# Attention with a gated feed-forward on one core: masked queries by transfers, a load count for spare matmuls, and traced transfer times

## The chip, the cores and the metric

The kernel runs on one core of a Trainium2 chip. Its engines are TensorE (PE in the profile; its weight loads are PEld), VectorE (DVE), ScalarE (ACT), GpSimd (POOL) and SyncE (SP), which here only issues transfers (DMAs). The metric is the time of one execution on the device in microseconds. Three runs of the kernel before took 1190.16, 1193.30 and 1193.92 us; their median is 1193.3.

## The reference

```python
x  = A_x                                   # [1, 2048, 512], bf16
xn = _layernorm(x)
qkv = (xn @ wqkv).reshape(B, S, 3, H, Dh)  # H = 32 heads of Dh = 16
scores = einsum("bhqd,bhkd->bhqk", q, k) * Dh ** -0.5
p = softmax(scores)                        # over 2048 keys
o = einsum("bhqk,bhkd->bhqd", p, v)
attention = o.reshape(B, S, D) @ wo        # wo: 512 x 512
h = silu(xn @ w1) * (xn @ w3)              # 512 -> 1792
feed_forward = h @ w2                      # 1792 -> 512
return x + attention + feed_forward
```

Inputs and output are bf16.

## The kernel before

**Units.** Queries are cut into 4 chunks of 512 and heads into 8 groups of 4. A chunk and a group are worked off in units of 256 queries, the first group in 128, 128, 256 and the last four groups in 128 each: 73 units. Four heads of 16 dimensions lie in four bands of 32 partitions of `QT` and `KT`; a band has 16 rows of data, then two rows that hold minus the maximum of each query (as a bf16 number and its rest) in `QT` and ones in `KT`; the other rows of `QT` are zero.

**First scores.** For each unit PE computes scores with queries on partitions (L1158, two heads of 512 keys at a time, each on 32 rows of the array), and DVE takes the maximum over each 512 keys (`tensor_reduce`, L1197, 128x1024 at a time). There are 1004 such reductions, and 10 more are done by another DVE operation (L1186) on a unit that ACT has helped to halve. PE has two places of 2 banks of PSUM for them, so it can be at most two ahead of DVE.

**Maxima to rows.** When the last reduction of a unit is done, POOL joins the partial maxima in six small operations (L1323 to L1330), writes minus the maximum and its rest into `Z` (L1300, L1302), and SP issues a transposing transfer `Zs<-Z` (L1346) and two transfers `QT<-Zs` (L1342) that put the rows into `QT`. After that the unit's second scores may begin.

**Second scores.** PE computes the scores again with keys on partitions and the maximum already subtracted, in one of two ways: one head on 32 rows of the array (L1447, four heads side by side), or "wide", all 128 rows, with a copy of the queries that is zero outside one head's band: `BD` (L661 and L665, inputs `BD,KT`). `BD` has two buffers, by the unit's parity, of four heads each. POOL makes it by multiplying `QT` with a column of `hmask` (L1284), one operation per head, after the rows of `QT` have landed. A wide matmul is used only where its mask is ready in the plan and PE's load is low, or where it fits.

**Exponentials and values.** ACT takes the exponential of a bank of 512 (L1472) or two banks at once (L1502) into `PT`. PE multiplies with the values and a column of ones (`PT,Vaug`, L665), which gives the unnormalized output and the sum; ACT copies it to `U` (L1566), and the normalization follows: transfer `Lc<-U` (L1587), reciprocal on POOL (L1591), transfer `rd<-Rc` to DRAM (L1596), transfer `R<-rd` back, spread over partitions (L1600), multiply on POOL (L1611).

**Other work of PE** is put between: transposes and projections of the inputs at the start, the feed-forward (tiles G and U, with three POOL operations per tile, L939 to L943), output sums OUT (OUTA and OUTB at the end), and spare matmuls (`fill_cand`), whose results nobody reads: they are placed where a running sum over the last 2 us, `heat`, is below `HEAT_FILL`. A weight per kind of matmul goes into it (`_HEAT_ROW`, `_HEAT_COL`, `_HEAT_FULL`). Where `heat` is below `HEAT_P1`, first scores are computed twice or three times over.

**The order** of every engine, SP's included, is written out by a planner inside `_build` before the program is made. It keeps a clock per engine, gives each item an `occ` (time on its engine) and a `lat` (time until others see its result; 2.3 us for a transfer unless another is given), and always takes the item that can begin first. For each 24 score tiles one of 53 sets of rule parameters (`SETS`) applies, by a list (`TUNE`). On the chip an engine follows its written order and waits at each item until what it needs is there; so a time that the planner has wrong does not make a wrong result, it makes a wait, and everything behind it on that engine waits too.

**The start**: x comes in four transfers, and layer norm's mean and variance are taken on DVE (`bn_stats`, L698) for the tile pairs marked "d" in `STATS`, on ACT (L688, L692) for those marked "a".

The clock per transfer, in the planner:

```python
def later_dma(fn, reads, writes, lat=2.3, cb=None, pred=None, occ=0.62):
    spq.append(_Item(fn, reads, writes, occ, lat, cb, pred))
```

Of the kernel before, what the change touches and what calls it, by code (L numbers as in the profile page):

```python
# [5 lines left out]
FP32 = mybir.dt.float32  # L6
# [8 lines left out]
_HEAT_ROW, _HEAT_COL, _HEAT_FULL = 0.794, 2.36, 2.16  # L15
# [22 lines left out]
class _Prog:  # L38
# [99 lines left out]
    def pe(self, fn, reads, writes, mode, groups, dur, name="", first=None):  # L138
# [19 lines left out]
        w = _HEAT_ROW * len(groups) if mode == "row" else _HEAT_FULL if self.pe_full else _HEAT_COL  # L158
        self.heat.append((start, start + dur, w))
# [98 lines left out]
def _build(nc, A_x, A_wqkv, A_wo, B_w1, B_w3, B_w2, out):  # L258
# [28 lines left out]
    AUG_LAT = 3.8  # L287
# [17 lines left out]
    BD_END = 4  # L305
    SPLIT_LO = 20
# [13 lines left out]
        dict(A_LEAD=0.85),  # L320
        dict(TOL=0.05),
        dict(TOL=0.15),
        dict(PV_LEFT=2),
        dict(PV_LEFT=8),
        dict(TEN_MID=2),
        dict(RELAX=0.05),
        dict(MIN_PIECE=2),
        dict(BD_NEAR=0.1),
        dict(BD_NEAR=0.5),
        dict(HEAT_FILL=0.0),  # L330
        dict(HEAT_FILL=2.0),
        dict(HEAT_WIDE=0.0),
# [6 lines left out]
        dict(A_LEAD=0.95, PV_LEFT=8, ROW_LEAD=0.43, PAIR_TEN=2),  # L339
        dict(ROW_LEAD=0.43, LAZY_GAP=0.02),  # L340
        dict(TOL=0.05, TEN_MID=2),
        dict(LAZY_GAP=0.02, ROW_LEAD=0.5, RELAX=0.05),
        dict(HEAT_P1=1.5, RELAX=0.05, PAIR_WAIT=0.1),
        dict(TEN_MID=2, ROW_LEAD=0.55),
        dict(HEAT_TILE=1.6, HEAT_FILL=3.0),
        dict(MIN_PIECE=2, MATE=0.0, WIDE_LEAD=0.7, HEAT_FILL=2.0),
        dict(RELAX=0.05, MATE=0.0, PAIR_WAIT=0.1, W_WAIT=0.1),
        dict(LAZY_GAP=0.02, TOL=0.15, HEAT_FILL=2.0, A_LEAD=0.69),
        dict(PAIR_WAIT=0.1, HEAT_FORCE=1.0, HEAT_WIDE=1.15, HEAT_P1=1.5),
        dict(LAZY_GAP=0.02, WIDE_LEAD=1.0, MATE=0.0),  # L350
        dict(TEN_MID=2, RELAX=0.05, LAZY_GAP=0.02, HEAT_WIDE=1.15),
        dict(MIN_PIECE=2, HEAT_FILL=2.0, LAZY_GAP=0.02, PAIR_WAIT=0.1),
        dict(HEAT_WIDE=1.4, PAIR_WAIT=0.1, PV_LEFT=8, HEAT_TILE=1.3),
        dict(MIN_PIECE=2, BD_NEAR=0.1, W_WAIT=0.1),
        dict(HEAT_TILE=1.3, MIN_PIECE=2),
        dict(BD_NEAR=0.1, HEAT_P1=0.0),
        dict(ROW_LEAD=0.55, RELAX=0.05, MATE=0.0),
        dict(ROW_LEAD=0.43, A_LEAD=0.85, HEAT_WIDE=0.0),
        dict(BD_NEAR=0.5, ROW_LEAD=0.5),
        dict(HEAT_TILE=1.6, PAIR_TEN=2, ROW_LEAD=0.55, HEAT_FILL=3.0),  # L360
        dict(HEAT_TILE=1.3, TOL=0.05, HEAT_FILL=1.15),
        dict(PAIR_TEN=0, WIDE_LEAD=1.0),
        dict(W_WAIT=0.1, TEN_MID=2, WIDE_LEAD=1.0),
        dict(ROW_LEAD=0.4, HEAT_FILL=2.0),
    )
    TUNE = (
# [73 lines left out]
    with ctx:  # L440
# [35 lines left out]
        hmask = sb("hmask", [128, 4], FP32)  # L476
# [64 lines left out]
        poolq = {k: [] for k in ("z", "ln", "nx", "split", "bd", "nrm", "ffn", "pad")}  # L541
# [23 lines left out]
        P.op("dve", lambda e: e.memset(hmask[:, :], 0.0), writes=[("hmask",)], occ=0.07)  # L565

        def head_masks(e):
            for j in range(4):
                ins = e.memset(hmask[32 * j:32 * j + 32, j:j + 1], 1.0)
            return ins  # L570
        P.op("dve", head_masks, writes=[("hmask",)], occ=0.26)
# [9 lines left out]
        NORM = "dddppppp"  # L581
        STATS = "ddddaaaa"
# [58 lines left out]
        wpad = {k: v.rearrange("p (c j) d -> p c (j d)", c=DC) for k, v in wpad.items()}  # L641
        poolq["pad"].append(_Item(lambda e: e.memset(Vaug[:, :, :, 16:17], 1.0), [],
# [36 lines left out]
        def ln_chunk(gi):  # L679
# [6 lines left out]
            if on_act:  # L686
                for t in tl:
                    act_stats.append(_Item(lambda e, t=t: e.activation(  # L688
                        a32[:, :], x_sb[:, t, :], ACTF.Identity, scale=1.0 / D, accum_out=mv[:, t, 0:1]),
                        [("PT", t)], [("a32",), ("mv", t)], 0.57, 0.7))  # L690
                for t in tl:
                    act_stats.append(_Item(lambda e, t=t: e.activation(  # L692
                        a32[:, :], x_sb[:, t, :], ACTF.Square, scale=-1.0, bias=mv[:, t, 0:1],
                        accum_out=mv[:, t, 1:2]),
                        [("PT", t), ("mv", t)], [("a32",), ("mv", t)], 0.66, 0.8, cb=lambda op: mv_done(op)))
# [575 lines left out]
        def bd_prep():  # L1271
# [10 lines left out]
            for j in (2, 3, 0, 1):  # L1282
                poolq["bd"].append(_Item(
                    lambda e, j=j: e.tensor_scalar(BD[:, u % 2, j, 0:nq], QT[:, qs, q0:q0 + nq], hmask[:, j:j + 1], 0.0,  # L1284
                                                   ALU.mult, ALU.add),
# [831 lines left out]
```

## Time and profile before

| | us |
|---|---|
| median of three runs | 1193.3 |
| the profiled execution's own time | 1192.82 |
| its span, first to last instruction | 1191.1 |
| DVE busy | 1167.3 |
| ACT busy | 1166.1 |
| PE busy | 1115.3 |
| POOL busy | 576.4 |

The span begins with the first instruction and ends with the last one; 1.7 us of the execution's time lie outside of it. A line such as `L1197 DVE ... part<-ps` is a group of instructions by source line, engine and tile, with its busy time, the mean length of one in ns, and the idle time of the engine just before them. Instructions of ACT and DVE overlap their neighbours a little, so the mean length is more than the distance from one to the next. In a table by stretches each row has the stretch, its length, busy time (and count) of PE, PEld, DVE, ACT and POOL, then the granted TensorE clock as a share of full speed, the share of the DMA engines and GB/s.

### The profile page before, as it was taken

The numbers are of one execution on the slowest core, as the hardware profiler recorded it, in microseconds if no ns is written. First come the engines' busy times: TensorE is split into PE (matmuls) and PEld (weight loads), VectorE is DVE, ScalarE is ACT, GpSimd is POOL, SyncE is SP. The second block draws the span as 40 slices with busy tenths as digits, with TensorE's granted clock in tenths as the row PEclk, the third lists the DMA queues.
The fourth block names the chain that finished last, engine by engine and source line by source line (L and its number), as shares of the span: only waits on it lengthen the run. The fifth ranks groups of instructions, "written<-read, shape, count | busy, mean of one in ns | idle before, by whom it ended". The sixth has DMA issues, their size and how long they took to land.

```text
span 1191.1 us, 35904 instructions
## 1 busy us (share of the span) xinstructions
PE 1115.3 (94%) x14863; PEld 531.2 (45%) x15011; DVE 1167.3 (98%) x1085; ACT 1166.1 (98%) x2259; POOL 576.4 (48%) x1200
## 2 busy tenths in 40 slices
PE   8999999999999999999999999999999999999998
PEld 4443444444444434433444443434444543356664
DVE  8999999999999999999999999999999999999995
ACT  7899999999999999999999999999999999999997
POOL 4457644545443375545354338554543337644430
PEclk9999999999999999999999999999999999999999
DMA  5423221111101121111101112111110112000000
GB/s 183 129 72 87 61 79 52 38 35 29 38 22 34 35 68 38 31 38 29 37 19 30 36 49 55 42 32 33 31 29 25 29 40 51 20 20 18 20 16 24
DMA packets 130790, 52.24 MB, mean 44 GB/s; under 512 B 99788, under 2 KB 130628, under 8 KB 130628
## 3 DMA queue, kind: packets, MB, share of 16 engines
q1 hardware_dynamic: 130628, 49.94, 16.3%
q8 instruction: 118, 1.93, 0.7%
q14 instruction: 44, 0.36, 0.1%
HBM read 38.67 MB, written 6.74 MB: 38 GB/s over the span
## 4 chain that ended last, share of the span: by engine, by line
ACT 56%; PE 23%; DVE 14%; DMA 4%; POOL 2%; issue 1%; SPq 0%; DVEq 0%; POOLq 0%
ACT PT L1472 41%; DVE part L1197 13%; PE ps L661 8%; ACT PT L1502 7%; PE ps L665 6%; PE ps L1447 4%; PE ps L1158 4%; DMA R<-rd 2%; ACT zg L960 1%; DMA rd<-Rc 1%; ACT ub L964 1%; ACT U L1566 1%; ACT th L954 1%; ACT kq L849 1%; POOL BD L1284 1%
## 5 line engine op out<-in xcount | busy, mean ns | idle before, releaser
L1197 DVE TENSOR_REDUCE part<-ps 128x2 f32<-128x1024 f32 x1004 | 1138.5, 1203 | 6.1 <-PE ps L1158 3.7
L1472 ACT ACTIVATE PT<-ps 128x512 bf16<-128x512 f32 x1706 | 918.3, 742 | 4.6 <-PE ps L1447 2.9
L1447 PE MATMUL ps<-QT,KT 32*128 32x256 bf16 (+1 forms) x3338 | 452.7, 258 | 9.6 <-ACT PT L1502 1.8
L1158 PE MATMUL ps<-KT,QT 32*128 32x512 bf16 x2140 | 431.7, 384 | 10.4 <-DVE part L1197 7.6
L1447 PEld LDWEIGHTS ps<-QT,KT 32*128 32x128 bf16 x3338 | 159.2, 92 | 163.0 <-ACT PT L1472 73.6
L665 PE MATMUL ps<-PT,Vaug 128*17 128x256 bf16 (+1 forms) x4672 | 202.4, 262 | 3.3 <-ACT PT L1502 0.9
L1502 ACT ACTIVATE PT<-ps 128x1024 bf16<-128x1024 f32 x171 | 193.3, 1157 | 0.0
L1591 POOL TENSOR_TENSOR Rc<-Lc,mone 128x8 f32<-128x8 f32 (+1 forms) x69 | 105.0, 1521 | 139.2 <-DMA Lc<-U 139.1
L1158 PEld LDWEIGHTS ps<-KT,QT 32*128 32x128 bf16 x2140 | 105.4, 91 | 143.5 <-issue 69.3
L661 PE MATMUL ps<-xnT,w 128*128 128x512 bf16 (+3 forms) x588 | 147.9, 316 | 11.1 <-ACT PT L1472 4.0
L661 PE MATMUL ps<-BD,KT 128*128 128x256 bf16 (+1 forms) x870 | 147.5, 263 | 9.2 <-ACT PT L1502 3.2
L1284 POOL TENSOR_SCALAR BD<-QT,hmask 128x256 bf16<-128x256 bf16 (+1 forms) x276 | 122.2, 457 | 65.6 <-DMA QT<-Zs 65.6
L665 PEld LDWEIGHTS ps<-PT,Vaug 128*17 128x17 bf16 x4672 | 92.9, 90 | 75.9 <-issue 53.9
L661 PE MATMUL ps<-xnT,ident 128*128 128x512 bf16 (+3 forms) x274 | 78.7, 325 | 12.6 <-ACT PT L1502 3.6
L661 PEld LDWEIGHTS ps<-BD,KT 128*128 128x128 bf16 x870 | 68.9, 98 | 43.7 <-ACT PT L1502 7.7
L1323 POOL TENSOR_TENSOR mx<-part 128x16 f32<-128x16 f32 (+1 forms) x67 | 14.1, 211 | 150.2 <-DVE part L1197 149.8
L665 PE MATMUL ps<-BD,KT 128*32 128x256 bf16 (+1 forms) x1856 | 82.9, 265 | 0.0
L661 PEld LDWEIGHTS ps<-xnT,w 128*128 128x128 bf16 x631 | 50.1, 97 | 73.5 <-issue 37.6
L661 PE MATMUL ps<-w,hT 128*128 128x128 bf16 (+3 forms) x330 | 77.3, 302 | 3.9 <-ACT U L1566 3.0
L943 POOL TENSOR_TENSOR hT<-a,t 128x512 bf16<-128x512 f32 x56 | 71.1, 1269 | 2.3
L941 POOL TENSOR_TENSOR a<-zg,ub 128x512 f32<-128x512 bf16 x56 | 64.6, 1153 | 5.1 <-ACT ub L964 4.9
L1611 POOL TENSOR_TENSOR wk_on<-U,R 128x256 bf16<-128x256 f32 (+1 forms) x36 | 22.9, 635 | 79.5 <-DMA R<-rd 79.5
(112 smaller groups left out, 776.9 us busy)
## 6 DMA issues: line engine op xcount, KB each, us to landing
w<-in_B_w_dram SPq DMA_DIRECT2D x112, 128.0 KB
R<-rd SPq DMA_DIRECT2D x55, 128.0 KB
QT<-qd SPq DMA_DIRECT2D x31, 128.0 KB
KT<-kd SPq DMA_DIRECT2D x28, 128.0 KB
PT<-in_A_x_dram SPq DMA_DIRECT2D x4, 512.0 KB
xr<-in_A_x_dram SPq DMA_DIRECT2D x16, 128.0 KB
out_dram<-osb SPq DMA_DIRECT2D x16, 128.0 KB
qd<-kq SPq DMA_DIRECT2D x15, 128.0 KB
```

The lines of the kernel that those rows point to most:

```text
L661: return e.matmul(bank(bk)[:, c0 + a:c0 + b], make_lhsT(0, 128), rhs_ap(0)[:, a:b], start=start, stop=stop, **kw)
L665: ins = e.matmul(bank(bk)[32 * i:32 * i + m, c0 + a:c0 + b], make_lhsT(i), rhs if (a, b) == (0, ncols) else rhs[:, a:b], start=start, stop ...
L941: q.append(_Item(lambda e: e.tensor_tensor(a32[:, :], zg[:, ss, :], ub[:, ss, :], ALU.mult), [("zg", ss), ("ub", ss)], [("a32",)], 1.1, 1.25))
L943: q.append(_Item(lambda e: e.tensor_tensor(hT[:, hslot(idx), :], a32[:, :], t1[:, :], ALU.mult), [("a32",), ("t1",)], [("hT", hslot(idx))] ...
L1158: ins = e.matmul(bank(2 * sl + i), QT[32 * j:32 * j + 32, qs, q * 128:(q + 1) * 128], KT[32 * j:32 * j + 32, g, c_ * 512:(c_ + 1) * 512], ...
L1197: redq.append(_Item(lambda e: e.tensor_reduce(dst, pair_ap.rearrange("p (a b) -> p a b", b=512), AX.X, ALU.max), writes, [("part", par, qt ...
L1284: lambda e, j=j: e.tensor_scalar(BD[:, u % 2, j, 0:nq], QT[:, qs, q0:q0 + nq], hmask[:, j:j + 1], 0.0, ALU.mult, ALU.add),
L1447: ins = e.matmul(bank(b)[:, i * nq:(i + 1) * nq], KT[32 * j:32 * j + 32, g, (k0 + i) * 128:(k0 + i + 1) * 128], QT[32 * j:32 * j + 32, qs, ...
L1472: expq.append(_Item(lambda e: e.activation(PT[:, sl, :], bank(b), ACTF.Exp, scale=SCALE), [("ps", b)], [("PT", sl)], _c_act(512), cb=cb, e ...
L1502: return _Item(lambda e: e.activation(PT[:, s0:s1 + 1:s1 - s0, :], ps8[:, b0:b1 + 1:b1 - b0, :], ACTF.Exp, scale=SCALE), [("ps", b0), ("ps ...
L1591: poolq["nrm"].append(_Item(lambda e: e.tensor_tensor(Rc[:, pp, 0:nl], Lc[:, pp, 0:nl], mone[:, 0:nl], ALU.pow), [("Lc", pp), ("mone",)], ...
L1611: poolq["nrm"].append(_Item(lambda e: e.tensor_tensor(onorm[ob][:, g, q0:q0 + nq], U[:, us, 0:nq], R[:, pp, 0:nq], ALU.mult), [("U", us)] ...
```

## The change

It has four parts.

1. **Masks.** `hmask` and POOL's multiplications are gone. `BD` is set to zero once by POOL; each head's band is then copied by a transfer from `QT` to `BD`, 32 partitions of 256 (or 128) bf16, with a planned latency of 2.1 us. The rest of a buffer stays zero.
2. **Load.** The weights of `heat` are replaced by a function that counts weight loads, tells value matmuls from others, and second scores from first.
3. **Transfer times** in the plan: transposing transfer 3.8 to 3.0, `QT<-Zs` 2.3 to 2.0, `Lc<-U` 2.3 to 2.0, `rd<-Rc` 2.3 to 1.7, `R<-rd` 2.3 to 3.6.
4. **Order.** Statistics of one more pair of x tiles go from ACT to DVE; ACT's choice among equals is by two new numbers; `SETS` (now 60) and `TUNE` are others.

```diff
-_HEAT_ROW, _HEAT_COL, _HEAT_FULL = 0.794, 2.36, 2.16
+def _heat(name, mode, groups, full, dur):
+    if mode == "row":
+        return (0.846 if name.startswith("p2") else 0.713) * len(groups)
+    n = 1 if full else 8 if name.startswith("w2") else 4
+    return (1.23 if name.startswith("PV") else 2.32) + 0.0284 * n / dur
...
-        w = _HEAT_ROW * len(groups) if mode == "row" else _HEAT_FULL if self.pe_full else _HEAT_COL
-        self.heat.append((start, start + dur, w))
+        self.heat.append((start, start + dur, _heat(name, mode, groups, self.pe_full, dur)))
...
-    AUG_LAT = 3.8
+    AUG_LAT = 3.0
...
-        STATS = "ddddaaaa"
+    STATS = "dddddaaa"
+    R_STAT = 2
+    R_SEC = 1
...
+        poolq["pad"].append(_Item(lambda e: e.memset(BD.rearrange("p s j n -> p (s j n)"), 0.0), [], [("BD0",)], 2.2,
+                                  pred=lambda: ("AUG", 0) in done))
...
             for j in (2, 3, 0, 1):
-                poolq["bd"].append(_Item(
-                    lambda e, j=j: e.tensor_scalar(BD[:, u % 2, j, 0:nq], QT[:, qs, q0:q0 + nq], hmask[:, j:j + 1], 0.0,
-                                                   ALU.mult, ALU.add),
-                    [("hmask",)] + qh_keys(qs, q0, nq) + qt_keys(qs, q0, nq, "QTr0") + qt_keys(qs, q0, nq, "QTr1"),
-                    [("BD", u % 2, j)], 0.12 + nq / 1000.0, cb=lambda op, j=j: done.add(("BD", u, j))))
+                later_dma(lambda e, j=j: e.dma_start(BD[32 * j:32 * j + 32, u % 2, j, 0:nq],
+                                                     QT[32 * j:32 * j + 32, qs, q0:q0 + nq]),
+                          [("BD0",)] + qh_keys(qs, q0, nq, (j,)) + qt_keys(qs, q0, nq, "QTr0") + qt_keys(qs, q0, nq, "QTr1"),
+                          [("BD", u % 2, j)], lat=2.1, cb=lambda op, j=j: done.add(("BD", u, j)))
...
-                            [("Zs", par)], qt_keys(qs, q0, nq, "QTr%d" % r),
+                            [("Zs", par)], qt_keys(qs, q0, nq, "QTr%d" % r), lat=2.0,
...
-                          cb=n2)
+                          lat=2.0, cb=n2)
...
-                          [("Rc", pp)], [("rd", pp)], cb=n4)
+                          [("Rc", pp)], [("rd", pp)], lat=1.7, cb=n4)
...
-                    .broadcast_to([4, 32, nq])), [("rd", pp)], RK, cb=n5)
+                    .broadcast_to([4, 32, nq])), [("rd", pp)], RK, lat=3.6, cb=n5)
...
-                    r = {"first": 0, "second": 1}.get(it.name, 2)
+                    r = {"first": 0, "second": R_SEC, "stat": R_STAT}.get(it.name, 2)
```

In the program that comes out, the 276 mask operations of POOL are 276 transfers; spare matmuls are 336 instead of 389 and wide score tiles 626 instead of 598; ACT takes 1720 single and 164 double banks of exponentials instead of 1706 and 171; the reductions stay at 1004 and 10.

More of the change, by code (lines that the diff above doesn't have):

```diff
@@ L305, in _build @@
     BD_END = 4
+    NORM = "dddppppp"
+    STATS = "dddddaaa"
+    R_STAT = 2
+    R_SEC = 1
     SPLIT_LO = 20
@@ L356, in _build @@
[L356 to L364, printed above, removed]
+        dict(HEAT_FILL=2.0, LAZY_GAP=0.02),
@@ new lines, in _build @@
+        dict(ROW_LEAD=0.55, MIN_PIECE=2),
+        dict(PV_LEFT=2, LAZY_GAP=0.02),
+        dict(HEAT_FILL=3.0, HEAT_WIDE=1.4, WIDE_LEAD=0.45, RELAX=0.05),
+        dict(TOL=0.05, W_WAIT=0.1),
+        dict(BD_NEAR=0.8, PAIR_TEN=2, RELAX=0.05, TOL=0.15),
+        dict(HEAT_FORCE=1.0, BD_NEAR=0.5, RELAX=0.05),
+        dict(MATE=0.0, PV_LEFT=2, A_LEAD=0.95, PAIR_WAIT=0.1),
+        dict(PAIR_WAIT=0.1, ROW_LEAD=0.55, MIN_PIECE=2),
+        dict(HEAT_P1=0.0, WIDE_LEAD=0.7, MATE=0.0),
+        dict(TEN_MID=2, TOL=0.05),
@@ new lines, in _build @@
+        dict(LAZY_GAP=0.02, HEAT_P1=1.5, MATE=0.0),
+        dict(ROW_LEAD=0.5, BD_NEAR=0.8, TOL=0.15, LAZY_GAP=0.02),
+        dict(RELAX=0.05, BD_NEAR=0.1, HEAT_P1=0.0, PV_LEFT=8),
+        dict(P2_MID=3, HEAT_FILL=2.0, RELAX=0.05, A_LEAD=0.6),
+        dict(SPLIT_LEAD=1.5, P2_MID=3, LAZY_GAP=0.02, ROW_LEAD=0.55),
+        dict(MIN_PIECE=2, HEAT_P1=1.2, A_LEAD=0.76, PV_LEFT=8),
+        dict(BD_NEAR=0.1, ROW_LEAD=0.36, TOL=0.1, HEAT_WIDE=1.15),
+        dict(FILL_SLIP=0.2, PAIR_TEN=2, PAIR_WAIT=0.2),
@@ new lines, in _build @@
+        dict(TEN_MID=1, ROW_LEAD=0.43, PAIR_TEN=2, FILL_SLIP=0.1),
+        dict(BD_NEAR=0.35),
+        dict(TOL=0.0, OUT_GATE=20, HEAT_TILE=1.3),
+        dict(FILL_SLIP=0.1),
+        dict(PAIR_DEPTH=4, W_WAIT=0.2, PV_LEFT=8, MIN_PIECE=1),
+        dict(TOL=0.1),
+        dict(OUT_GATE=8, FILL_SLIP=0.0),
+        dict(HEAT_P1=0.0, URG_WAIT=0.15, HEAT_TILE=1.3, FILL_SLIP=0.1),
+        dict(ROW_LEAD=0.43, HEAT_FORCE=1.0),
+        dict(A_LEAD=0.55),
+        dict(BD_NEAR=0.35, ROW_LEAD=0.5, FILL_SLIP=0.2),
@@ L365, in _build @@
+        dict(WIDE_LEAD=0.7, ROW_LEAD=0.36),
+        dict(RELAX=0.1, PAIR_DEPTH=2, P2_MID=3, SPLIT_LEAD=1.5),
+        dict(HEAT_P1=1.2, HEAT_TILE=1.3, HEAT_FILL=3.0),
+        dict(PAIR_TEN=0, AGAIN=1, P2_MID=4, URG_WAIT=0.05),
     )
     TUNE = (
[6 rows of a table removed]
[6 rows of a table added]
     )
@@ L475, in _build @@
         mx = sb("mx", [128, 2, 8, 2], FP32)
-        hmask = sb("hmask", [128, 4], FP32)
         negm = sb("negm", [128, 2, 8], FP32)
@@ L540, in _build @@
         dveq = []
-        poolq = {k: [] for k in ("z", "ln", "nx", "split", "bd", "nrm", "ffn", "pad")}
+        poolq = {k: [] for k in ("z", "ln", "nx", "split", "nrm", "ffn", "pad")}
         spq = []
@@ L564, in _build @@
         P.op("dve", lambda e: e.memset(wq_last[:, :, :], 0.0), writes=[("wq7",)], occ=0.3 * NPADQ)
[L565 to L571, printed above, removed]
         P.op("dve", lambda e: e.memset(bank(7), 0.0), writes=[("ps", 7)], occ=0.5)
@@ L1999, in pick_pool @@
             b = None
-            for k in ("z", "ln", "nx", "split", "bd", "nrm", "ffn", "pad"):
+            for k in ("z", "ln", "nx", "split", "nrm", "ffn", "pad"):
                 q = poolq[k]
```

31 lines of the change are left out of this document (6 added, 25 removed), and 12 rows, old and new, of the table TUNE.

## The prediction

> **What bounds the kernel now.** Read the page first: busy shares and the groups of instructions.
>
> ```profile
> PE 1115.3 (94%) x14863; PEld 531.2 (45%) x15011; DVE 1167.3 (98%) x1085; ACT 1166.1 (98%) x2259; POOL 576.4 (48%) x1200
> ...
> ACT 56%; PE 23%; DVE 14%; DMA 4%; POOL 2%; issue 1%; SPq 0%; DVEq 0%; POOLq 0%
> ...
> L1197 DVE TENSOR_REDUCE part<-ps 128x2 f32<-128x1024 f32 x1004 | 1138.5, 1203 | 6.1 <-PE ps L1158 3.7 <-PE ps L1447 2.1
> ...
> L1284 POOL TENSOR_SCALAR BD<-QT,hmask 128x256 bf16<-128x256 bf16 (+1 forms) x276 | 122.2, 457 | 65.6 <-DMA QT<-Zs 65.6
> ```
>
> VectorE (DVE) and ScalarE (ACT) are both 98% busy, and the chain names ACT first. The table by stretches decides: the first reduction of scores starts at 13.56, the last ends at 1168.10.
>
> ```profile
> 0.00:13.56 13.56, 10.56 (x97) 7.90 (x98) 8.84 (x31) 6.13 (x15) 5.17 (x20) 1.00 0.88 293
> 13.56:1117.09 1103.53, 1039.59 (x13437) 482.39 (x13573) 1102.06 (x985) 1096.05 (x2127) 553.56 (x1134) 1.00 0.17 42
> 1117.09:1143.90 26.81, 23.69 (x504) 15.93 (x506) 23.20 (x22) 23.30 (x50) 10.47 (x35) 0.94 0.09 19
> 1143.90:1168.10 24.20, 23.33 (x408) 14.78 (x409) 24.20 (x23) 24.00 (x49) 6.79 (x13) 1.00 0.08 16
> 1168.10:1191.10 23.00, 18.10 (x426) 10.18 (x429) 8.97 (x27) 16.63 (x24) 0.45 (x1) 0.97 0.09 28
> ```
>
> The fifth number of a row is DVE's busy time (after length, PE and PEld). For 1103.5 us DVE lacks 1.5 us. So the time is a head of 13.6, a row of 1014 large DVE operations that neither kernel changes, the few waits in it, and a tail of 23.0. GpSimd (POOL), which the change unloads by 122 us, is half idle: that by itself is worth nothing. What can move is head, waits, tail. DVE's timeline shows the longest waits:
>
> ```profile
> 824.78 36.27 DVE L1197 TENSOR_REDUCE part<-ps 128x2 f32<-128x1024 f32 x32 [0.72 <-PE ps L1447]
> ...
> 1109.18 14.91 DVE L1197 TENSOR_REDUCE part<-ps 128x2 f32<-128x1024 f32 x13
> 1124.79 1.23 DVE L1197 TENSOR_REDUCE part<-ps 128x2 f32<-128x1024 f32 x1 [0.69 <-PE ps L1158]
> 1126.66 1.23 DVE L1197 TENSOR_REDUCE part<-ps 128x2 f32<-128x1024 f32 x1 [0.65 <-PE ps L1447]
> 1128.64 11.45 DVE L1197 TENSOR_REDUCE part<-ps 128x2 f32<-128x1024 f32 x10 [0.75 <-PE ps L1447]
> ...
> 1140.07 2.35 DVE L1197 TENSOR_REDUCE part<-ps 128x2 f32<-128x1024 f32 x2
> 1143.90 6.93 DVE L1197 TENSOR_REDUCE part<-ps 128x2 f32<-128x1024 f32 x6 [1.48 <-PE ps L1158]
> ```
>
> Undisturbed, 32 reductions take 36.27 us; a single one is 1.23 long, so they start (36.27 - 1.23) / 31 = 1.13 us apart. From 1109.18 to 1143.90 there are 27 of them, 27 x 1.13 = 30.5, and one small maximum of about 0.1; they took 34.7. So **4.1 us are lost in this one zone**, in the units of 128 queries at the end. The chain there, in order of time:
>
> ```profile
> 1128.59 3.55 DMA R<-rd
> ...
> 1138.88 3.32 DMA R<-rd
> ...
> 1142.28 0.45 POOL wk_on L1611
> 1142.73 0.18 POOL Z L1300
> ```
>
> The normalizing multiply L1611 waits for R; the two Z operations (L1300, L1302) behind it on POOL's queue feed PE, which waits, and DVE behind PE. The planner had entered 2.3 us for R; 3.3 to 3.6 passed. The other wait, near 1123, lies in SyncE's (SP's) queue:
>
> ```profile
> 1120.41 0.58 SPq L1600 DMA_DIRECT2D R<-rd  x1
> 1121.04 1.08 SPq L1342 DMA_DIRECT2D QT<-Zs  x2
> ```
>
> ```profile
> 1123.61 0.38 PE L1447 MATMUL ps<-QT,KT 32*128 32x128 bf16 x4 [0.83 <-DMA QT<-Zs]
> ```
>
> QT's rows stand behind R's issue, and PE waits 0.83 us for them.
>
> **The change part by part.** *Transfer times and the masks off POOL.* In the order written out for the changed kernel, the multiply that waits for R stands in this zone behind the Z pair, not among the steps that lead to it; QT's rows are issued ahead of rd and R; no mask operation stands between. Late R then holds only Rc and the next unit's maxima, over 7 us later. I count the 4.1 us as gone but for 0.7: **-3.4**. If a latency grows again, up to 4.1 come back; if all goes, 0.7 more is saved.
>
> *The 276 mask copies become 276 transfers on SP*, 16 KB each (8 KB in short units), issued in fours after QT's rows land. The trace has none. Nearest are QT's rows:
>
> ```profile
> L1342 SPq DMA_DIRECT2D QT<-Zs x134: 497/520/632, 58.9 to 1140.1; - x134
> ...
>   PE ps L1447: 0.8, 1
> ```
>
> Issue 0.52 us each, so SP issues 276 x 0.52 = 144 us more over 1191, four per unit of 9 to 18 us. Landing: the pair issued from 1121.04 released PE at 1123.61, so at most 2.6 us for both; the other end is R's 3.55. I take 2.0, as this is also a copy inside SBUF. What it costs when late: 134 such transfers made PE wait 0.8 us in all, 0.006 each; 276 more give 1.6, and I let a third reach DVE: **+0.5**. Bounds: 0 if masks always land ahead; 7 by the rival below. No gain, since PE never waited for POOL's masks long enough to show.
>
> In front of that, SP's queue holds what stands behind a mask that waits for QT's landing: rd, R and the weight loads. In the short units I count ten issues per unit, with two landings waited for, within 9.05 us (8 x 1.13): 10 x 0.5 and two landings of about 2 make 9, so this queue is nearly full there.
>
> The Trainium skill, "DMA: Bandwidth & Descriptors", Rules for kernel authors, speaks against this part: many small transfers are to be joined, since below 64 KB one pays mostly overhead. The rows agree, since at 2 KB nearly all of the time is fixed; but by its rule too the cost lies in latency, and here it counts only where a mask lands after its first matmul.
>
> POOL gains one memset of BD early (its nearest row, twice the size, ran 3.5 us on the page, so an estimate of 1.8), behind which only Z of unit 1 stands.
>
> *Spare matmuls.* They fall from 389 to 336, and repeats of score matmuls from 2160 to 2086 instructions. PE is not the bound, so fewer saves nothing directly; what matters is the granted clock (after POOL's busy time in a row):
>
> ```profile
> 817.69:821.10 3.41, 2.47 (x29) 0.88 (x23) 3.41 (x4) 3.41 (x7) 1.75 (x2) 1.00 0.03 11
> 821.10:824.52 3.42, 3.42 (x38) 1.26 (x34) 2.70 (x3) 2.72 (x6) 1.69 (x8) 0.50 0.02 5
> 1121.48:1124.89 3.41, 2.44 (x28) 1.45 (x26) 2.72 (x4) 2.80 (x6) 1.62 (x6) 1.00 0.09 20
> 1124.89:1128.30 3.41, 3.25 (x86) 2.32 (x87) 2.35 (x2) 2.37 (x5) 2.07 (x6) 0.50 0.09 15
> ...
> 1141.96:1145.37 3.41, 2.10 (x29) 1.55 (x30) 1.93 (x3) 1.91 (x5) 3.01 (x8) 1.00 0.01 0
> ```
>
> Twice before the end the clock was halved for 3.41 us, each time after a stretch of that length with PE busy 2.4 to 2.5; a stretch of 2.10 was not punished, so it is not busy time alone. A halved stretch cost DVE 3.42 - 2.70 = 0.7, or 1.06 together with waits: 0.9 each. The second followed from the wait near 1123 and is in the 4.1. By matmul sizes, with the change's own weights, I compared the load between scores three reductions apart: the lowest place in the order of before lies at reductions 705 to 712, which is the halved place (13.56 + 710 x 1.138 = 821); the changed order has two places lower still (479 to 484) and two about equal (728, 950). A place must also coincide with a stretch. I expect 1.5 halved stretches in place of one: 1.5 x 0.9 - 0.7 = **+0.6**; ends -0.7 (none) and +4 (five).
>
> The Trainium skill, "TensorE: Matmul & The Clock Gate", Part 1, says that the clock falls after a window of about 3.4 us in which PE idles. The row at 817.69 differs: PE was busy 2.47 of 3.41 and the clock fell. By that page this term would be -0.7, and the sum 1.3 lower, which is part of the clean case below.
>
> *Head.* One more pair of x tiles goes from ACT to DVE.
>
> ```profile
> 10.47 1.25 DVE L698 BATCH_NORM_STATS2 U<-PT 128x6 f32<-128x512 bf16 x2
> 11.64 0.16 DVE L701 BATCH_NORM_AGGREGATE U<-U 128x2 f32<-128x6 f32 x1
> ...
> 13.56 27.33 DVE L1197 TENSOR_REDUCE part<-ps 128x2 f32<-128x1024 f32 x24 [1.05 <-PE ps L1158]
> ```
>
> Two statistics are 11.64 - 10.47 = 1.17 and an aggregate 0.08: 1.25 ahead of the first reduction, into a hole of 1.05; a second aggregate follows it: 0.2 + 0.1 = **+0.3**, from 0 (if the hole is longer) to 1.3. ACT loses the work but is not waited for then. The four dropped hmask writes ran before any data had come: nothing.
>
> *Tail.*
>
> ```profile
> 1171.30 1.58 ACT L1472 ACTIVATE PT<-ps 128x512 bf16<-128x512 f32 x3 [0.76 <-PE ps L1447]
> ```
>
> ```profile
> 1187.54 0.68 DVE L1062 TENSOR_TENSOR osb<-ps,th 128x512 bf16<-128x512 f32 x1
> 1188.13 0.68 DVE L1062 TENSOR_TENSOR osb<-ps,zg 128x512 bf16<-128x512 f32 x1
> ```
>
> Both orders leave 37 score tiles after the last reduction's matmuls, but 20 fewer other groups (147 against 127 on PE), so ACT's 0.76 wait may go; and only one output sum, not two, stands behind the last normalization: 1188.13 - 1187.54 = 0.6 less. **-1.3**, between -2 and +0.5.
>
> **Sum.** +0.3 - 3.4 + 0.5 + 0.6 - 1.3 = -3.3 on the profiled execution's 1192.82 (its span of 1191.1 and 1.7 around it): 1189.5. The runs' median is 1193.3 (1190.16 to 1193.92), so that execution is typical. A difference of 0.3%, 3.6 us, is about what a measurement of this kernel can tell from no change: 1189.7 and 1196.9 are the bounds.
>
> **Rivals.**
> *Clean*: no halved stretch (-1.3 more), the tail at its good end (-0.7), the zone wholly free (-0.7): 1186.8. Against it: the lower places in the order.
> *The clock takes it back*: five halved stretches, 3.5 more than forecast, x 0.9 = +3.2: 1192.7. For it: 53 fewer spare matmuls; against: with each matmul's weight load counted, the load in most places is no lower.
> *It doesn't do what it says*: the zone's waits stay, since R is still 3.5 us and SP's queue now holds four masks ahead of it: 1189.5 + 3.4 = 1192.9. Against: what waited there no longer stands behind R.
> *Late masks, slower*: in the changed order PE's second scores begin 10 to 21 reductions after the last reduction of a 256-query unit (13 to 24 before); in nine units with masks the lead is 12 or less (13.6 us). If masks land 1.5 later than planned there (R's 3.55 in place of 2.0) the matmul that needs them holds up PE's queue, the next scores with it: about the 0.83 seen above, 9 x 0.8 = +7.5: 1197. It decides once a mask lands after its first matmul; below that it costs nothing.
>
> **How the numbers follow.** Forecast 0.52 (1186.8 to 1192; six tenths of it below 1189.7), clean 0.12, clock 0.12, doesn't do it 0.06, late masks 0.18 (to 1205, if twice as many units wait; of it 0.02 under 1196.9). Faster 0.33 + 0.12 = 0.45; same 0.19 + 0.12 + 0.06 + 0.02 = 0.39; slower 0.16. The range runs from 1185.5 (the clean case with head and masks at nothing, 1186.0, less the half microsecond by which the profiled execution stands off the median) to 1198, which takes in the late masks at their price and leaves out their worse half.
>
> **What would show it.** Right: no idle time of DVE over 0.5 us between 1100 and the last reduction; PE waits for BD's transfers under 2 us in all; zero to three halved stretches ahead of the end; last reduction's end to span's end near 21.7. Wrong: a row "PE <- DMA BD" of many times, then late masks; many clock drops at 0.50 with PE busy about 2.5 before them, then the clock; a first reduction after 14.5, then the head was mis-sized.

## The result and the profile after

Eight runs of the changed kernel took 1194.81 to 1201.62 us, median 1197.95; eight of the kernel before beside them 1190.16 to 1193.92, median 1191.62. The ratio is 1.0055 (95% interval 1.004 to 1.0069): the change costs about 6.6 us where I had forecast a gain of 3.3. The profiled execution of the changed kernel took 1194.81, so it is the lowest of its eight; span 1193.1.

The page first: busy shares, the chain, DVE's reductions and the wide second scores.

```profile
PE 1113.7 (93%) x14891; PEld 527.2 (44%) x15026; DVE 1167.4 (98%) x1083; ACT 1164.2 (98%) x2259; POOL 460.7 (39%) x925
...
ACT 66%; PE 20%; DVE 12%; issue 1%; DMA 1%; POOL 0%; ACTq 0%; SPq 0%; POOLq 0%
...
L1205 DVE TENSOR_REDUCE part<-ps 128x2 f32<-128x1024 f32 x1004 | 1138.4, 1211 | 8.4 <-PE ps L1454 7.4
...
L669 PE MATMUL ps<-BD,KT 128*128 128x256 bf16 (+1 forms) x834 | 147.4, 266 | 13.8 <-DMA BD<-QT 6.2
```

POOL lost 116 us of work and DVE, the bound, kept its own. The new line is the last: matmuls that read `BD` stood 6.2 us for a transfer `BD<-QT`. The table by stretches says where (stretch, length, busy time of PE, PEld, DVE, ACT, POOL, then granted clock, share of the DMA engines, GB/s):

```profile
0.00:14.00 14.00, 11.41 (x93) 8.34 (x94) 9.84 (x28) 6.11 (x14) 5.30 (x21) 1.00 0.90 293
14.00:50.89 36.89, 35.65 (x281) 15.95 (x285) 36.79 (x35) 31.41 (x71) 21.33 (x36) 1.00 0.30 83
50.89:62.53 11.64, 5.07 (x38) 2.05 (x38) 4.49 (x4) 4.61 (x8) 1.70 (x8) 0.56 0.75 168
62.53:1117.09 1054.56, 993.21 (x13071) 458.50 (x13186) 1053.94 (x942) 1051.28 (x2036) 417.53 (x820) 1.00 0.17 43
1117.09:1143.66 26.57, 25.53 (x469) 16.55 (x467) 26.57 (x24) 26.57 (x56) 8.94 (x29) 1.00 0.11 24
1143.66:1171.13 27.47, 25.98 (x601) 16.37 (x606) 27.47 (x28) 27.33 (x58) 5.11 (x12) 1.00 0.07 16
1171.13:1193.09 21.96, 16.90 (x355) 9.45 (x357) 8.30 (x25) 16.84 (x23) 0.84 (x2) 0.98 0.10 29
```

In the third row DVE works 4.49 of 11.64 us, the clock is at 0.56, and the DMA engines are 75% busy, against 7 to 17% in the rows behind. Every other row from the first reduction to the last is full: the 4.1 us that the kernel before lost after 1117 are gone in this execution. The chain of waits through that place, and SP's queue at the same time:

```profile
48.09 9.09 DMA BD<-QT
57.18 0.14 issue
57.32 0.80 PE ps L669 x5
```

```profile
46.76 0.45 SPq L659 DMA_DIRECT2D w<-in_B_w_dram  x1
47.31 1.71 SPq L1291 DMA_DIRECT2D BD<-QT  x2
49.22 0.90 SPq L845 DMA_DIRECT2D KT<-kd  x2
50.16 1.15 SPq L1291 DMA_DIRECT2D BD<-QT  x2
```

```profile
58.70 1.23 DVE L1205 TENSOR_REDUCE part<-ps 128x2 f32<-128x1024 f32 x1 [6.58 <-PE ps L1454]
```

A mask of unit 1, 8 KB, took 9.09 us to land. In the whole trace the median over 276 mask transfers, from the start of the issue to the semaphore event of the landing, is 1.80. Ahead of this one SP had issued L659, the load of w2, 1792 KB in one transfer; it landed after 9.8 us. By the distance of 1.13 us between reductions DVE lost 6.7 us at 50.9 and 1.2 us on the next three, at half clock. In the kernel before the same load was issued at 44.6 and landed in 7.4 us, and nothing was issued behind it until 51.5, close to its landing: the masks were made by POOL.

So the first theory was: **the load**, issued ahead of unit 1's masks, is the loss. Its rivals were **the clock** (fewer spare matmuls) and **late masks** in general.

### The profile page after: what moved, and what is told of

Its sections match the earlier page's. It is cut to its first block, busy times and chain, and to the rows that moved or that the text cites. A ratio compares the mean times of both kernels' runs of the same rounds, so it can differ in the third digit from the quotient of the medians.

```text
span 1193.1 us, 36078 instructions
## 1 busy us (share of the span) xinstructions
PE 1113.7 (93%) x14891; PEld 527.2 (44%) x15026; DVE 1167.4 (98%) x1083; ACT 1164.2 (98%) x2259; POOL 460.7 (39%) x925
## 4 chain that ended last, share of the span: by engine, by line
ACT 66%; PE 20%; DVE 12%; issue 1%; DMA 1%; POOL 0%; ACTq 0%; SPq 0%; POOLq 0%
ACT PT L1479 46%; DVE part L1205 11%; ACT PT L1509 10%; PE ps L669 8%; PE ps L673 4%; PE ps L1454 4%; PE ps L1166 4%; ACT zg L968 2%; ACT th L962 2%; ACT ub L972 2%; ACT U L1573 1%; DMA BD<-QT 1%; ACT kq L857 1%; ACT RB L1273 1%; PE ps L1815 1%
## 5 line engine op out<-in xcount | busy, mean ns | idle before, releaser
L1479 ACT ACTIVATE PT<-ps 128x512 bf16<-128x512 f32 x1720 | 928.5, 750 | 8.8 <-PE ps L669 6.3
L1454 PE MATMUL ps<-QT,KT 32*128 32x256 bf16 (+1 forms) x3322 | 447.8, 257 | 10.4 <-ACT PT L1509 1.5
L1166 PE MATMUL ps<-KT,QT 32*128 32x512 bf16 x2066 | 419.4, 384 | 11.6 <-DVE part L1205 7.6
L1509 ACT ACTIVATE PT<-ps 128x1024 bf16<-128x1024 f32 x164 | 187.8, 1177 | 0.7 <-PE ps L1454 0.6
L669 PE MATMUL ps<-xnT,w 128*128 128x512 bf16 (+3 forms) x606 | 151.7, 313 | 13.1 <-ACT PT L1479 4.2
L673 PE MATMUL ps<-BD,KT 128*32 128x256 bf16 (+1 forms) x2064 | 93.6, 265 | 0.3 <-ACT kq L857 0.2
L669 PEld LDWEIGHTS ps<-BD,KT 128*128 128x128 bf16 x834 | 64.8, 98 | 50.3 <-ACT PT L1479 11.1
L669 PE MATMUL ps<-w,hT 128*128 128x512 bf16 (+3 forms) x332 | 78.1, 304 | 4.1 <-ACT U L1573 2.6
L669 PE MATMUL ps<-xnT,ident 128*128 128x512 bf16 (+3 forms) x238 | 67.3, 318 | 12.4 <-DVE part L1205 4.9
L947 POOL TENSOR_SCALAR t<-th 128x512 f32<-128x512 bf16 x56 | 34.7, 620 | 85.8 <-ACT th L962 84.9
```

Of the source, the lines that this page charges most:

```text
L669: return e.matmul(bank(bk)[:, c0 + a:c0 + b], make_lhsT(0, 128), rhs_ap(0)[:, a:b], start=start, stop=stop, **kw)
L673: ins = e.matmul(bank(bk)[32 * i:32 * i + m, c0 + a:c0 + b], make_lhsT(i), rhs if (a, b) == (0, ncols) else rhs[:, a:b], start=start, stop ...
L947: q.append(_Item(lambda e: e.tensor_scalar(t1[:, :], th[:, ss, :], 1.0, 1.0, ALU.mult, ALU.add), [("th", ss)], [("t1",)], 0.62, 0.72))
L1166: ins = e.matmul(bank(2 * sl + i), QT[32 * j:32 * j + 32, qs, q * 128:(q + 1) * 128], KT[32 * j:32 * j + 32, g, c_ * 512:(c_ + 1) * 512], ...
L1454: ins = e.matmul(bank(b)[:, i * nq:(i + 1) * nq], KT[32 * j:32 * j + 32, g, (k0 + i) * 128:(k0 + i + 1) * 128], QT[32 * j:32 * j + 32, qs, ...
L1479: expq.append(_Item(lambda e: e.activation(PT[:, sl, :], bank(b), ACTF.Exp, scale=SCALE), [("ps", b)], [("PT", sl)], _c_act(512), cb=cb, e ...
```

## The experiments

The kernels are numbered e1 to e13. All but e12 keep the order that the planner wrote out for the changed kernel and edit it afterwards, so that every engine keeps its list but for the edit. Line numbers shift by a few lines from kernel to kernel. "Lost" below is DVE's time over 1.13 us per reduction.

**The changed kernel once more (e1).**

> The changed kernel as it is, for its spread and a second profile. Load theory (unit 1's four mask transfers land 8.4 to 9.6 us after their issue instead of 1.8 because the 1.8 MB load of w2 was issued just ahead of them, and PE stands 6.2 us): median 1196 to 1200, and in the profile one wait of PE for BD of 6 to 11 us near 51 us, longer where the run is longer; nothing else over 1 us. Clock theory (fewer spare matmuls, so the clock is halved more often): runs that are longer have more halved stretches between 100 us and the end. Late-masks theory: the waits for BD are many and small.

Median 1199.4 (1197.14 to 1204.09), ratio 1.0059 (1.0042 to 1.0077). Its waits (us in all, times, longest):

```profile
DVE part L1205 <- PE ps L1454: 14.4, 9, 8.3
...
PE ps L669 <- DMA BD<-QT: 10.4, 2, 8.0
```

The wait near 51 is there again, 8.0 us long, and a second one that I had not expected, at the end:

```profile
1148.45 1.23 DVE L1205 TENSOR_REDUCE part<-ps 128x2 f32<-128x1024 f32 x1 [2.73 <-PE ps L1454]
1150.07 3.71 DVE L1205 TENSOR_REDUCE part<-ps 128x2 f32<-128x1024 f32 x3 [0.40 <-PE ps L1454]
```

This execution, the slowest of the six with 1204.09, lost 3.8 us after 1100, and 2.9 near 1065 with the clock halved. The first profile, of the fastest of eight, had shown neither.

**The load as a whole at other places, and half of it (e2, e3, e4).**

```diff
-            later_dma(lambda e: e.dma_start(w2[:, :, :], w2_v), [], [("w2",)], lat=12.0)
+            later_dma(lambda e: e.dma_start(w2[:, :, :], w2_v), [], [("w2",)], lat=12.0, cb=P.late.append)
...
+        sp, ld = P.ops["sp"], P.late[0]
+        sp.remove(ld)
+        sp.insert(54, ld)      # 41 in the second kernel
```

> The same order on every engine, only the w2 load is issued 23 places later on SP's queue, behind the masks of units 1 and 2. Load theory: no wait of PE for BD over 0.5 us near 51; the 6.7 us of DVE's wait and about 1.2 us of halved clock behind it go: 1194.8 - 7.9 = 1186.9, between 1185.5 and 1189, so 0.3 to 0.5 per cent under before. Clock theory and late-masks theory: within 1 us of the changed kernel run beside it.

> As the run before, but the load goes only 10 places back, just behind unit 1's masks and wo and ahead of unit 2's maxima (Zs<-Z, then QT<-Zs, then unit 2's masks). Load theory: unit 1's masks land about 2 us after their issue, and the wait at 51 goes; Zs<-Z of unit 2, issued right behind the load, lands about 6 to 9 us late instead of 2.4, and if unit 2's second scores come within that, a smaller wait for QT or BD shows near 60 to 70. 1187 to 1191. Clock and late-masks theories: as the changed kernel.

> The load is cut in two: 7 of its 14 blocks (0.9 MB) stay ahead of unit 1's masks, the other 7 are issued behind unit 2's masks. Load theory: the delay goes with the bytes ahead. The whole took 9.8 us; with some 2 us fixed, half takes about 6, so unit 1's masks land near 53 instead of 57 and PE stands about 2.3 us instead of 6.2: 1194.8 - 3.9 = 1190.9, less about 1 if the clock isn't halved: 1188.5 to 1192. If only the place in the queue counted and not the bytes, the wait would stay at 6. Clock and late-masks theories: as the changed kernel.

All three expectations missed: medians 1201.01, 1200.95 and 1200.73, ratios 1.0071 (1.0058 to 1.0084), 1.0059 (1.0038 to 1.008), 1.0065 (1.0046 to 1.0085), like the changed kernel itself. Yet in none of their profiles was the clock or a row of many small waits the reason: the wait had moved with the load. Behind unit 2, the first transfer after the load was `rd`. SP has 24 semaphores for its transfers and takes them in turn, and this `rd` had the load's:

```profile
64.80 8.16 DMA w<-in_B_w_dram
...
73.02 1.95 DMA rd<-Rc
```

SP stood until the load had landed, R and QT came late, and PE waited 6.0 us for QT at unit 3. That was my own placing, and another mechanism than the one under test. Behind unit 1 it was the one under test, on the next transfer in line, with 4.5 us of wait for QT:

```profile
54.11 0.43 SPq L660
54.54 0.04 issue
54.58 8.64 DMA Zs<-Z
```

The half load answers the question of size: unit 1's mask took 5.18 us to land instead of 9.09, PE's wait was 2.1 and DVE lost 2.0 at 50.3 (2.3 expected). But the other half, issued behind unit 2, cost 3.2 at unit 3 and 1.6 more at half clock. All three lost 3.2 to 5.2 us after 1100 as well.

**The load in pieces (e5).** Its 14 blocks of 128 KB go into holes of SP's queue, one semaphore of their own for all.

```diff
+            gaps = [sp[k] for k in (73, 89, 113, 132, 148, 166, 167, 187, 200, 216, 217, 229, 241, 255)]
+            sp.remove(ld)
+            for c, o in enumerate(gaps):
...
+                op.fn = lambda e, c=c: e.dma_start(w2[:, c, :], w2_v[:, c, :])
+                sp.insert(sp.index(o) + 1, op)
```

> The changed kernel, with the w2 load cut into its 14 blocks of 128 KB, each put into a hole of SP's queue between 94 and 297 us (w2 is first read near 350). The runs before showed that the whole load costs 5 to 8 us wherever it stands among unit 1 to 3's transfers. Load theory: no wait of PE for BD, QT or Zs over 1 us before 300; the 6.7 to 8.4 us and 1.2 to 1.5 us of halved clock go: 1198.7 - 9 = 1189.7 if the waits near 1140 stay at about 3 us; 1188.5 to 1192. Rival (the wait only moves on, because ACT or another engine is as late): 1197 and over, with new waits elsewhere.

Median 1189.18 (1186.45 to 1195.4), ratio 0.9992 (0.9977 to 1.0008). Against e1's 1.0059, each taken against the kernel before run beside it, that is 0.67%, 8.0 us, and by the two intervals taken together (the root of the sum of their squared halves) about 2.8 to either side. Around 51 DVE now runs without a gap. One wait for a transfer is left among PE's longer waits, at unit 3 near 80, with which this execution lost 2.9 us in all, most of it at half clock:

```profile
43.45 37.60 DVE L1233 TENSOR_REDUCE part<-ps 128x2 f32<-128x1024 f32 x33
```

```profile
PE ps L1482 <- DMA QT<-Zs: 0.9, 1, 0.9
```

The load theory holds for the larger part, by its removal and by its dose. The traces give its price at its own place as 7.9 us in "after" and about 10 in e1; the 8.0 of the medians also holds what the executions lose elsewhere. After 1100 this execution lost no more than 0.2.

**The end: the unread masks, R's place, masks doubled (e6, e7, e8).** For the waits after 1100 I had two theories. One: SP's queue is full in the units of 128 queries. The other: masks land late there whatever the queue holds.

```diff
+            read = {id(d) for o in P.ops["pe"] for d in o.deps}
+            drop = [o for k, o in P.tag.items() if k[0] == "BD" and id(o) not in read]
+            P.refit(drop)
```

> As the run before, and the 34 of 276 mask transfers whose copy no matmul reads are left out (15 of them in units 60 to 68); every other instruction stands as it was. Queue theory of the waits near 1140 (in the units of 128 queries SP's ten issues, with the loop rd, masks, R, multiply, reciprocal, rd, take 7.8 to 9.5 us of a unit's 9.05): one or two issues of 0.6 fewer in most of these units, so the waits there fall from 3 to 5 us to 0.5 to 2: 1 to 3 us less than e5. Lateness theory (masks land late because of other traffic, whatever the queue holds): as e5 within 1 us.

> As the run before, and in units 60 to 68 with four masks R is issued behind the second mask instead of the fourth, and the load xr of 128 KB near 1130 goes behind Zs and Lc. Queue theory: the loop is another 0.5 to 1.2 us shorter in those units, waits after 1100 under 0.7 us in all: 1186 to 1188.5, the best version. Lateness theory: as e5 within 1 us, or worse, since two masks now go out later.

> As e5, and behind each of the 32 mask transfers of units 61 to 68 stands one more transfer of the same size (32 partitions of 128 bf16 from ident into ones_t, which nobody reads any more). Nothing waits for them but the next of their kind. Queue theory: four more issues of 0.6, 2.5 us in a loop of about 8.3 that may take 9.05: (8.3 + 2.5 - 9.05) x 8 = 14 us over e5, between 8 and 20, as waits of PE for QT and BD between 1080 and 1160. Lateness theory: the engines move 8 KB more per transfer and are idle nearly all of the time, so within 2 us of e5.

Without the 34 unread masks: median 1187.52 (1186.31 to 1189.71), ratio 0.998 (0.997 to 0.999). With R ahead and the load xr moved back as well: 1187.58 (1185.94 to 1191.11), 0.9981 (0.9972 to 0.999), so that edit adds nothing that can be told. Masks doubled in units 61 to 68: 1209.42 (1205.16 to 1212.84), ratio 1.0158 (1.0133 to 1.0182), 20 us over e5, with these among its waits:

```profile
DVE part L1233 <- PE ps L1482: 14.6, 16, 3.7
...
PE ps L697 <- DMA BD<-QT: 5.3, 3, 3.0
```

32 transfers of 8 KB cost 20 us at the end (14 expected, 20 at most), the halved clock behind the waits included, while the DMA engines were 9% busy from 1100 to 1150. So SP's queue can cost that much there, as the queue theory says. SP's own list shows how full it is without them. First one unit of "after", from `Zs<-Z` to the next, then the same place in e6's order:

```profile
1119.79 1.59 SPq L1353 DMA_TRANSPOSE Zs<-Z  x1
1121.43 0.60 SPq L1594 DMA_DIRECT2D Lc<-U  x1
1122.56 1.09 SPq L1349 DMA_DIRECT2D QT<-Zs  x2
1124.39 0.35 SPq L1603 DMA_DIRECT2D rd<-Rc  x1
1124.91 2.46 SPq L1291 DMA_DIRECT2D BD<-QT  x4
1127.42 0.58 SPq L1607 DMA_DIRECT2D R<-rd  x1
1128.04 0.81 SPq L996 DMA_DIRECT2D xr<-in_A_x_dram  x1
1128.90 1.14 SPq L1353 DMA_TRANSPOSE Zs<-Z  x1
```

```profile
1116.36 0.58 SPq L1635 DMA_DIRECT2D R<-rd  x1
1116.99 0.47 SPq L1024 DMA_DIRECT2D xr<-in_A_x_dram  x1
1119.51 1.14 SPq L1381 DMA_TRANSPOSE Zs<-Z  x1
```

The eleven issues of "after" take 7.5 of the unit's 9.1 us, and the next `Zs<-Z` follows the last of them at once. In e6 SP has issued everything 2.05 us ahead of it, in the units beside it 2.55 and 0.97: it has time to spare. How late `Zs<-Z` goes out, in us after the start of one fixed reduction for each row, worked out from the traces (67 such transfers, counted from 0):

```
        after     e1     e2     e3     e4     e5     e6     e8
no 58    0.72  -0.06   0.28   1.15   0.46   0.63  -0.09   0.50
no 60    0.96   1.57   1.81   2.03   1.28   1.41  -1.06   3.10
no 62    0.69   1.38   1.31   1.23   0.99   0.89  -2.13   6.26
no 64    1.02   3.83   3.83   3.69   2.09   1.03   0.13   5.72
no 66    0.12   5.00   4.48   3.22   2.49   0.12   0.13   4.83
```

In the changed order the loop from `rd` over masks, R, multiply and reciprocal back to `rd` takes about as long as a unit. In "after" and e5 it just kept up; in e1 to e4 it fell behind by 2 to 5 us, did not catch up, and DVE lost 3.2 to 5.2. What pushed it over in the one execution and not in the other is not shown: late masks alone don't tell, for "after" had one of 4.71 us near 1117 and e5 one of 4.99 near 1111, and neither lost anything there. Nor is it excluded that the w2 load has a part in it: of the six profiles with the load whole or in halves five lost 3.2 to 5.2 us after 1100, and of the five with it in 14 pieces, apart from e8 and e10, none lost over 0.4; but only e5 of these five has all the masks on SP. Whether leaving out the unread masks is worth something in the median isn't settled by the intervals of e5 and e6, which overlap. It fits the queue theory that four of e5's eleven runs took over 1191 us, and one of the 20 of e6 and e7.

**Masks by POOL again (e9)**, in e6's order.

> The order of e6 (load in pieces, unread masks left out), but the 242 masks are made by POOL again, as in the kernel before: each multiplication stands in POOL's list at the planned moment at which QT's rows have landed; PE, ACT and DVE keep their order, SP has no mask transfers. If the transfers as such are what the change pays for (queue theory in its strong form): SP's loop at the end has six issues instead of eight to ten, so at most 2 us less than e6, 1185.5 to 1187. If they pay for themselves: POOL stands for QT's rows four times per unit ahead of maxima, Z and R's multiply, the loop at the end goes through POOL as well, and waits of 1 to 4 us show after 1050 as in the kernel before: 1188.5 to 1192.

Median 1190.02 (1187.11 to 1193.97). The kernel before took 1192.69 beside it and 1190.36 beside e6, so the ratio decides: 0.998 (0.9968 to 0.9992), the same as e6's, and 0.2 us lost after 1100. POOL now stands for QT's rows, and SP for less:

```profile
POOL BD L1331 <- DMA QT<-Zs: 58.5, 27, 5.9
```

So, within the 2 us that these intervals can tell, the transfers as such are neither gain nor loss, once the load is out of their way and unread ones are left out; what is left of the gain belongs to the order and the other parts of the change. Both expectations missed: no gain by taking them from SP, and no waits at the end by giving them to POOL.

**No spare matmuls (e10).**

> e6 without its spare matmuls (all 336 that fill_cand placed, about 0.2 us each; their results are read by nobody); the instruction behind each inherits its waits, all else stands. Clock theory: PE's load falls under what keeps the clock in many places; a halved stretch of 3.4 us cost DVE 0.7 to 1.06 before, so with 15 to 60 such stretches 1200 to 1240. Rival (spare matmuls do nothing here, and 53 fewer could not matter): 1186.5 to 1188.5 and zero to three halved stretches ahead of the end.

Median 1249.37 (1241.73 to 1250.65), ratio 1.0465 (1.0439 to 1.0491). The granted clock in 40 slices, first e10, then e6:

```profile
PEclk9999999877899999888879999899888999865989
```

```profile
PEclk9999999999999999999999999999999999999999
```

28 times the clock was halved, for 218 us in all: the spare matmuls are worth some 60 us (1249.4 against 0.998 x 1192.7), more than I had expected. The run leaves out 290 of them and not 336: 46 of the plan's 336, and of the 389 of the kernel before, stand in the first 12 us, ahead of the first scores (L1815, input `ones_t`), and these stayed. That the spare matmuls of the changed kernel mostly suffice is seen in e6, whose profile, of the fastest of its nine runs, has no halved stretch ahead of the end.

**An attempt at a better version (e11).**

> e6 with two edits, for the best version. QT's rows of unit 3 are issued ahead of R, which waits for rd's landing, near 75: the PE wait of 0.4 to 1.1 us for QT near 80 and the halved clock that followed it in one profile go. And each spare matmul planned between 1035 and 1062 is issued three times: two of nine profiles of the changed order had the clock halved for 10.2 us from there, after a stretch with PE busy 2.93 of 3.41, and lost 2.9 us. Expected 1186.0 to 1187.3 (e6 1187.5), no run over 1189.5, no wait for QT near 80, no halved stretch between 90 and 1180. If these places don't matter: as e6 within 0.3 us.

The expectation missed: 1196.91 (1193.67 to 1199.29), ratio 1.0036 (1.0025 to 1.0047). The wait for QT near 80 gave way to one of 1.0 us for BD. No stretch ahead of the end was halved, but with three matmuls for one PE itself became late there, and DVE lost 4.8 us between 1037 and 1068 (the profiled execution took 1193.76; what the slower ones lost besides is not shown):

```profile
1044.58 5.84 DVE L1233 TENSOR_REDUCE part<-ps 128x2 f32<-128x1024 f32 x5 [0.71 <-PE ps L1482]
1051.14 8.22 DVE L1233 TENSOR_REDUCE part<-ps 128x2 f32<-128x1024 f32 x7 [0.72 <-PE ps L1482]
```

**The kernel before with its load in pieces (e12).**

> The kernel before with the w2 load cut into 14 blocks put into holes of SP's queue between 99 and 306 us. My prediction took that load as hidden there, since no transfer of masks stood behind it: then 0.5 us to either side of before, and in the profile no other loss in the first 300 us than before. If the kernel before pays for it as well, 2 to 8 us less. Its profile is also a second look at the waits near 1120 to 1144: 3 to 5 us again if they belong to the order, 0 to 2 if they came from that one execution.

Median 1191.83 (1190.73 to 1194.52), ratio 0.9996 (0.9986 to 1.0007): the load had cost nothing there that could be told, 1.7 us at the most. And its waits at the end came back, 6.2 us in this execution:

```profile
1123.31 1.23 DVE L1225 TENSOR_REDUCE part<-ps 128x2 f32<-128x1024 f32 x1 [0.91 <-PE ps L1186]
...
1142.99 2.40 DVE L1225 TENSOR_REDUCE part<-ps 128x2 f32<-128x1024 f32 x2 [1.97 <-PE ps L1186]
```

**The load from ACT's queue (e13).** This was for the mechanism: a place in SP's queue, or shared engines.

```diff
+            def with_load(e, f=at.fn):
+                e.dma_start(w2[:, :, :], w2_v).then_inc(dma_sems[_NDMA_SEMS], 16)
+                return f(e)
+            at.fn = with_load
```

> The changed kernel, with the w2 load whole and at the same moment, but issued by ACT (ahead of its instruction planned for that time) instead of SP; all else stands. It costs ACT one issue of about 0.5 us. Queue-order theory (a transfer stands behind those issued before it on its own queue): unit 1's masks share the engines with the load but don't stand behind it, land 2 to 5 us after their issue, and PE's wait for BD near 51 is 0 to 2 us: 1190 to 1194. Shared-engine theory (1.8 MB keeps all engines busy whatever queue it came from): the masks land 8 to 9 us late again and PE stands about 6 us: 1197 to 1200.

Between the two: median 1195.58 (1194.38 to 1197.56), ratio 1.0034 (1.0021 to 1.0047). Unit 1's mask:

```profile
47.00 5.81 DMA BD<-QT
52.81 0.14 issue
52.95 0.74 PE ps L701 x5
```

It landed after 5.81 us instead of 9.09, and the one before it after 5.94 instead of 9.56, while the load itself took 13 (45.6 to 58.6) instead of 9.8, and DVE lost 3.0 instead of 6.7. But unit 1's other two masks, issued at 49.28 and 49.85, still took 8.26 and 8.38 us, against 8.83 and 8.44. So with the load on a queue of its own the first two masks get in between, but all four still land late: most of the delay stays though nothing of the load stands ahead of them on SP, as it would if the engines are shared. The Trainium skill, "DMA: Bandwidth & Descriptors", Queues, rings and completion order, says that a transfer engine takes descriptors of one ring in their order and goes round between the rings of different queues; the first two masks in "after" and e13 agree with it (9.56 and 9.09 against 5.94 and 5.81), and the later two gained next to nothing.

## Why the prediction was wrong, step by step

**Masks, +0.5: the step that failed.** I priced "what it costs when late" by the row of `QT<-Zs`, 0.006 us per transfer, bounded a landing by R's 3.55, and asked what stands behind a mask in SP's queue. I did not ask what stands ahead of it. The median landing is 1.80 (I took 2.0), and that term is right for nearly all of 276; but four masks stood behind 1.8 MB and took 8.4 to 9.6. Measured: 8.0 us, give or take 2.8, in place of 0.5 (e5 against e1), halved clock included. The load was in the trace of before, harmless; it became harmful because the change made PE's inputs transfers that are issued behind it. The rival "late masks", 1197, came nearest in time, and the range, which went up to 1198 for its sake, just takes in the median of 1197.95; but the wait was one of 6 to 8 us and not nine of 0.8, so that nearness is luck.

**Zone, -3.4.** In the profiled execution 4.1 us went, as the step said (all but 0.7). That late R was their cause is read from the trace of before; no run tried it by itself. And e1 to e4 and e13 lost 3.2 to 5.2 us at the same place; in e1 to e4, by the table above, `Zs<-Z` went out late from the full queue of SP, not behind R in POOL's. I had counted that queue, "ten issues per unit", "nearly full", and then charged nothing for it. The count "10 x 0.5" was short, too: ten of the eleven issues above, without xr, take 6.7 us, since a mask takes 0.6 and the transposing transfer 1.1 to 1.6. A loop with no slack costs nothing in one execution and 4 us in the next.

**Halved stretches, +0.6.** None ahead of the end in the profiles of "after" and e6, apart from those behind a wait. In e5 there was one, 3.4 us long, near 1040. In e1 and e7, 10.2 us at half clock and 2.9 us lost, each time from reduction 917 or 918 on:

```profile
1050.80:1054.21 3.41, 2.93 (x40) 1.74 (x36) 3.41 (x4) 3.33 (x7) 0.04 (x1) 1.00 0.13 32
1054.21:1057.62 3.41, 3.41 (x75) 2.17 (x76) 3.13 (x3) 2.47 (x4) 2.91 (x8) 0.50 0.02 5
```

That is e7: PE busy 2.93 of 3.41, more than in the rows that I had read before, and still punished, so busy time alone is no measure of the load. I had not named this place. One that I had named, reductions 479 to 484, showed in e9 (559.85 to 566.68), behind a stretch with PE busy 3.07 of 3.42. Counted in stretches of 3.4 us, that is nine in the twelve profiles with all spare matmuls, where I had expected 1.5 in each: the step was on the high side, and the spare matmuls that are left suffice nearly everywhere. What I gave as repeats of score matmuls, 2160 and 2086, are about all of the first scores (2140 and 2066 in the traces), repeats included.

**Head, +0.3.** First reduction at 14.00 against 13.56; twelve more profiles of this order have it from 13.37 to 14.24. No cost that can be told from that spread.

**Tail, -1.3.** 21.96 instead of 23.0, and 21.93 to 22.05 in eleven other profiles of this order (24.5 in e2, at half clock); e12, with the order of before, had 22.98. So -1.04, and the step was right.

**The sum.** Without the load's 8.0 us the changed kernel stands at 0.9992, and at 0.998 without the unread masks: 1.0 to 2.4 us under before, against 3.3 forecast. A part of that gap is that I took one execution for typical: the profiled ones of the kernel before, 1192.82, and of e12, 1193.5, lie above the medians of their runs, 1191.62 and 1191.83, so the loss at the end that could be won back is probably smaller in a median run; no trace of one shows it. The lowest ratio is 0.998 of the kernel before, in e6 and e9, and with e7 beside them.

## What to carry to other kernels

When small transfers take over work that an engine did, read what the queue issues just ahead of them, not only what waits behind: here one large load there made the transfers behind it land in 8.4 to 9.6 us instead of 1.8, and moving it as a whole moved the wait. Cut it into pieces and put them into holes of the queue. Count the issues per unit against the unit's time, and where little is left, charge for it, since one profile may show nothing.

## What the runs showed that I had not expected

Small transfers landed late in step with packets of the queues marked "instruction". In the trace of "after", 548 small transfers (BD, QT's rows, Lc, rd) were sorted by two things: whether such a packet started from 0.5 us before to 2.5 us after the issue, and whether a transfer of 64 KB or more, R included, was in flight 0.3 us after it. Over 0.7 us later than their median were:

```
                      no instruction packet    instruction packet
no load in flight         0 of 224                56 of 144
load in flight           27 of 117                29 of 63
```

With the packets' times shifted by 5 us, the first row reads 40 of 214 and 16 of 154; without R among the large transfers, 16 of 279 and 63 of 160. In e3, the stretch 1137.5 to 1142.5, in which a mask took 4.24 us, held one such packet of 16 KB among 586 small ones:

```profile
q1 hardware_dynamic: 586, 0.13, 12.0%
q8 instruction: 1, 0.02, 1.4%
```

The trace does not say which engine a packet ran on, and no run changed these packets, so this is an association, not a shown cause. The Trainium skill, "DMA: Bandwidth & Descriptors", Queues, rings and completion order, states that a transfer's semaphore event is written only after every earlier write of the same transfer engine, across its queues; by that a 16 KB packet could hold up a small transfer of another queue, which no run here shows.
